# Opening chain, riding routing products, zero fill and first layer norm of an attention, expert and feed-forward kernel

## The chip, the cores and the metric

One core of a Trainium2 chip. The metric is the device time of one execution in microseconds (us). The kernel before was run three times: 1099.04, 1099.73 and 1099.8 us, median 1099.73.

## What is computed

Sparse attention on q, k, v of shape (4, 8, 576, 64), then a mixture of experts in which a token keeps the expert of the one before it, then a layer norm and a feed-forward layer with a residual:

```python
scores = scale * np.matmul(q, k.transpose(0, 1, 3, 2))
thresh = np.max(scores, axis=-1, keepdims=True) - tau
scores = np.where(scores >= thresh, scores, -1000000000.0)
...
            if s == 0 or local_gate[b, s] < 0.5:
                e = fresh_e
            else:
                e = prev_e if prev_e >= 0 else fresh_e
...
            h = np.maximum(x[b, s] @ w1[e], 0.0)
            out[b, s] = p[e] * (h @ w2[e])
...
    xn = (x - mu) / np.sqrt(var + 1e-06) * g_ln
    ch = np.maximum(xn @ w_ch1, 0.0) @ w_ch2
    return (x + ch).astype(np.float32)
```

`x` is the output of attention, laid out as (4, 576, 512). There are 8 experts with weights of 512 x 1024 and 1024 x 512, and the feed-forward layer is 512 x 2048 and back.

## The kernel before

The order of every engine's work is the order in which the program issues it (of the constants ahead of the loads, an order that a scheduler chose; with the change, as issued there too). All products are made of halves: a float is split into two half-precision parts, and three or four matmuls of the parts stand for one.

**Attention** runs over 16 pairs of heads (`p`), 4 pairs to a batch, with 9 items (`j`) to a pair: 144 items of 128 rows of keys or queries. One pass of the main loop (`while it < NI or later`) takes one item through several stages at once. Item `g = it + 13` gets its row maximum (`mx`, on DVE, from scores that `s_mm` put into PSUM); when all nine of a pair have theirs, `th_parts` (POOL) and `th_rows` (PE, ACT) turn maxima into thresholds; item `it + 1` gets the transposed scores less the threshold (`t_mm`, PE, into a tile `s`), item `it` its exponential (`ex`, ACT), item `it - 1` the comparison with the threshold (`mask`, DVE) and the split into halves (`hilo`, ACT and POOL); `pv` multiplies with v, `norm` divides, `store` writes to `x_d` in DRAM. What else is to happen stands in the table `later`, by the number of the pass (`at`): loads, scaling and splitting of the next q and k (`scale_qk`, `split_qk`), their DMA transpose (`prep_t`), the copy `ku` with the halves exchanged (`prep_u`), and the **weight steps**: 11 of the 16 pieces of the feed-forward weights are loaded, narrowed on DVE, scaled on ACT and split, one piece in two halves to a pair (`ffn_steps`, `FO`).

**Routing.** After a pair, `gate` transposes its output and multiplies it with the gate weights, through the one PSUM bank `ps_t`; after the fourth pair of a batch `route` follows, some 30 small DVE instructions with four small products on PE between them (`row`, `kb`, `R`, `A`), each in the same bank. `step_bg` advances this by two steps a pass. As `th_rows` wants the same bank, `settle` runs whatever holds it to its end first.

**The experts** begin while the last batch is routed: `early_work` does a unit "a" of tokens of the first three batches. A **unit** is one or two tiles of 128 tokens of one expert: `gather`, `t_unit` (transposes), `s1_unit` twice or four times (first product, ReLU), `s2_unit` (second product, scaled into `yb` and scattered into `ys_d` with its row number). `ys_d` is filled with zeros beforehand (L1119 to L1126). Weights come in pieces of 512 KB through five buffers `stg`: `more` issues the load, `drip` has ACT and DVE split a loaded piece. After the units of the eight experts come six dynamic ones (`u` from 8 on).

**The feed-forward layer** works on 256 rows at a time: `f_load`, `f_norm`, `f_split`, `f_x` (a DMA transpose on ACT's queue that gives `nT`), then `halve`, which does `f_1` eight times or `f_2` twice, between the dynamic units and then on its own to the end.

Engines: PE multiplies, DVE and ACT work from PSUM and SBUF, POOL from SBUF; SP issues most DMAs.

## Time and profile before

| What | Value |
|---|---|
| Median of three runs | 1099.73 us |
| The profiled execution's own time | 1096.08 us |
| Its span | 1094.3 us |
| Busy share of the span: PE, DVE, ACT, POOL | 92%, 59%, 46%, 36% |
| Granted clock of PE, mean | 0.958 |

Times in a profile count from the span's start. A busy time says that an engine had an instruction running; the arrow behind a row of the timeline names what ended the idle time before it. [...] SPq, ACTq and POOLq are the queues of an engine that issue DMAs; their duration is that of the issuing, not of the transfer. [...]

### The profile page before, as it was taken

How to read it: one execution, taken by the hardware profiler on the slowest of the kernel's cores; microseconds unless marked ns; L12 is line 12 of the kernel's file. 1: busy time of each engine (PE TensorE's matmuls, PEld its weight loads, DVE VectorE, ACT ScalarE, POOL GpSimd, SP SyncE). 2: the span in 40 equal slices, each digit the busy share in tenths (PEclk: the TensorE clock that was granted, in tenths of full speed). 3: DMA queues.
4: the chain of work that ended last, by engine and by line, in shares of the span. 5: the costliest groups of instructions: out<-in, count | busy, mean ns of one | idle time of the engine just before them, and what ended most of it. 6: DMA issues, size and time to landing. Idle time of an engine off the chain costs nothing. (4 is left out here: it accounts for less than half of the span.)

```text
span 1094.3 us, 23622 instructions
## 1 busy us (share of the span) xinstructions
PE 1003.1 (92%) x9888; PEld 738.5 (67%) x9888; DVE 644.8 (59%) x1130; ACT 505.3 (46%) x792; POOL 393.1 (36%) x403
## 2 busy tenths in 40 slices
PE   3799997999799896799999979999999999999995
PEld 1477885788588775576677658576677577576572
DVE  4698889799876852879778767456231231231220
ACT  3587885788477563455567545344111021121110
POOL 4498986789587572025122220100100000000000
PEclk9899998999799997699999989999999999999998
DMA  7546535454433029768879876556011111111100
GB/s 174 144 105 177 146 96 137 107 148 111 107 69 70 21 50 231 237 205 277 270 255 323 259 240 203 151 161 172 25 40 40 30 50 39 30 49 40 29 11 22
DMA packets 126917, 138.23 MB, mean 126 GB/s; under 512 B 69706, under 2 KB 91210, under 8 KB 126800
## 3 DMA queue, kind: packets, MB, share of 16 engines
q1 hardware_dynamic: 101536, 117.71, 38.3%
q0 software_dynamic: 4960, 14.17, 3.6%
q10 hardware_dynamic: 20304, 4.74, 2.5%
q8 instruction: 79, 1.29, 0.5%
q14 instruction: 38, 0.31, 0.1%
HBM read 100.17 MB, written 19.94 MB: 110 GB/s over the span
## 5 line engine op out<-in xcount | busy, mean ns | idle before, releaser
L438 POOL TENSOR_TENSOR hl<-em,hl 128x576 f16<-128x576 f32 x128 | 169.9, 1329 | 58.8 <-ACT hl L437 52.2
L1030 PE MATMUL a<-nT,fw 128*128 128x256 f16 x1728 | 190.1, 273 | 0.0
L1043 PE MATMUL y<-fw,hid 128*128 128x512 f16 x864 | 187.9, 379 | 0.0
L1030 PEld LDWEIGHTS <-fw 128*128 128x128 f16 x1728 | 169.1, 98 | 21.5
L1043 PEld LDWEIGHTS <-hid 128*128 128x128 f16 x864 | 84.5, 98 | 100.4
L138 DVE SCALAR_TENSOR_TENSOR w<-stg,w 128x1024 f16<-128x1024 f32 x112 | 134.2, 1221 | 26.5 <-ACT w L137 17.0
L425 ACT ACTIVATE e<-s,t 128x576 f32<-128x576 f32 x144 | 106.2, 737 | 83.8 <-PE s L420 82.5
L1033 ACT ACTIVATE hid<-a 128x512 f16<-128x512 f32 x72 | 42.7, 593 | 212.7 <-PE a L1030 210.9
L1048 POOL DMA_INDIRECT out_dram<-xf x18 | 18.9, 1051 | 311.9 <-DVE xf L1047 311.9
L942 PE MATMUL y<-w,hid 128*128 128x512 f16 x528 | 120.2, 385 | 6.6 <-ACT hid L925 5.7
L921 PE MATMUL a<-xT,w 128*128 128x128 f16 (+1 forms) x1536 | 124.0, 243 | 2.1 <-DVE w L138 0.9
L382 DVE TENSOR_REDUCE mc<-sm 128x1 f32<-128x576 f32 x140 | 105.1, 751 | 34.7 <-PE sm L378 33.8
L137 ACT ACTIVATE w<-stg 128x1024 f16<-128x1024 f32 x112 | 114.6, 1051 | 18.3 <-DMA x_d<-xc 8.9
L921 PEld LDWEIGHTS <-w 128*128 128x128 f16 x1536 | 114.2, 100 | 12.5 <-issue 1.6
L431 DVE SCALAR_TENSOR_TENSOR em<-s,e 128x576 f32<-128x576 f32 x144 | 107.5, 747 | 20.5 <-POOL hl L438 13.2
L378 PE MATMUL sm<-qkt 128*128 128x288 f16 (+1 forms) x312 | 81.4, 306 | 34.3 <-DMA qkt<-nat 17.3
L1034 DVE SCALAR_TENSOR_TENSOR hid<-a,hid 128x512 f16<-128x512 f32 x72 | 49.6, 688 | 100.0 <-ACT hid L1033 100.0
L1047 DVE SCALAR_TENSOR_TENSOR xf<-y,xf 128x512 f32<-128x512 f32 x18 | 12.5, 692 | 146.8 <-PE y L1043 146.8
L942 PEld LDWEIGHTS <-hid 128*128 128x128 f16 x528 | 51.6, 99 | 68.2 <-ACT hid L925 6.6
L437 ACT ACTIVATE hl<-em 128x576 f16<-128x576 f32 x128 | 87.0, 679 | 21.3 <-DVE em L431 20.8
L415 PE MATMUL s<-qkt 128*128 128x288 f16 (+1 forms) x320 | 92.9, 298 | 3.6 <-DVE em L431 3.3
L378 PEld LDWEIGHTS <-qkt 128*128 128x128 f16 (+1 forms) x640 | 58.3, 109 | 56.2 <-issue 21.3
(272 smaller groups left out, 1840.3 us busy)
## 6 DMA issues: line engine op xcount, KB each, us to landing
stg<-in_moe_w_dram SPq DMA_DIRECT2D x112, 512.0 KB
stg<-in_moe_w_ch_dram SPq DMA_DIRECT2D x32, 512.0 KB
ys_d<-zero SPq DMA_DIRECT2D x2, 2308.5 KB
xf<-ys_d SPq DMA_DIRECT2D x9, 513.0 KB
ku<-qkt SPq DMA_DIRECT2D x30, 144.0 KB
rawq<-in_q_dram SPq DMA_DIRECT2D x8, 512.0 KB
rawk<-in_k_dram SPq DMA_DIRECT2D x8, 512.0 KB
vraw<-in_v_dram SPq DMA_DIRECT2D x8, 512.0 KB
```

Source lines behind the costliest of these rows:

```text
L137: nc.scalar.activation(out=dst[:, 0, n], in_=t, func=AF.Copy, scale=scale)
L138: nc.vector.scalar_tensor_tensor(out=dst[:, 1, n], in0=t, scalar=scale, in1=dst[:, 0, n], op0=ALU.mult, op1=ALU.subtract)
L378: mm(o[:, W0 + 288 * c:W0 + 288 * c + 288], ops[p, "q"][0][:, n], y, start=(k == 0), stop=(k == 1))
L382: nc.vector.tensor_reduce(out=mcs[p % 2][:, j:j + 1], in_=mms.pop((p, j))[:, W0:W0 + 576], op=ALU.max, axis=AX.X)
L415: mm(o[:, W0 + 288 * c:W0 + 288 * c + 288], (kt, ku)[k][:, n], y, start=(k == 0), stop=False)
L425: nc.scalar.activation(out=e, in_=mst[p, j][:, W0:W0 + 576], func=AF.Exp, bias=t0, scale=SC)
L431: nc.vector.scalar_tensor_tensor(out=em, in0=ps[:, W0:W0 + 576], scalar=0.0, in1=e, op0=ALU.is_ge, op1=ALU.mult)
L438: nc.gpsimd.tensor_tensor(out=hl[:, 1], in0=em, in1=hl[:, 0], op=ALU.subtract)
L921: nc.tensor.matmul(ps[:, f, :], t1[:, a, c, fc], x[:, h, i:i + N // 128, c, :], start=(n == 0), stop=(n == 11))
L942: nc.tensor.matmul(ps, hid[:, x, f, 128 * i:128 * i + 128], t2[:, a, f, :], start=(n == 0), stop=(n == 23))
L1030: nc.tensor.matmul(ps[:, f, :], fw1[:, a, c, fc], x[:, h, :, c, :], start=(n == 0), stop=(n == 11))
L1043: nc.tensor.matmul(ps, hid[:, x, f, ts_], fw2[:, a, f, :], start=(n == 0), stop=(n == 47))
```

## The change

*Opening.* q and k of the first pair alone are loaded first, k on ACT's queue (`load_pair`); constants are made on POOL instead of DVE, and the memsets stand behind the loads (`blanks`, new; its lines were in the setup before); 14 matmuls of ones run meanwhile; `start_qk` splits k on DVE and q on ACT and DVE, and PE transposes both. The loop starts with 9 passes of lead, and in four passes of pair 0 a second maximum is taken, which brings the lead to 13. `th_parts(0)` is on DVE. Pair 1 still goes through a DMA transpose, and its `ku` is copied on DVE.

```diff
+    ctx.enter_context(tc.manual_schedule())
...
+        def load_pair(nm, n, e):
+
+            src = {"q": q, "k": k, "v": v}[nm][0]
+            e.dma_start(
+                out=raws[nm][:, n].rearrange("p (h r) d -> p h (r d)", h=2)[:, :, 0:4 * D],
+                in_=src[2 * n:2 * n + 2, 0:512].rearrange("h (p r) d -> p h (r d)", r=4))
...
-            if p:
+            if p > 1:
...
+
+        def start_qk():
+
+            V = nc.vector
+            nat = tr_p.tile([128, 18, 128], F16, name="qkt")
+            scale_qk(0, "q", False)
+            rq, rk = (raws[nm][:, 0, 0:9] for nm in "qk")
+            V.tensor_scalar(out=rk, in0=rk, scalar1=16.0, scalar2=None, op0=ALU.mult)
+            nc.scalar.activation(out=nat[:, 0:9, 0:64], in_=rq, func=AF.Copy)
+            V.tensor_copy(out=nat[:, 9:18, 0:64], in_=rk)
+            V.tensor_tensor(out=nat[:, 9:18, 64:128], in0=rk, in1=nat[:, 9:18, 0:64], op=ALU.subtract)
+            V.tensor_tensor(out=nat[:, 0:9, 64:128], in0=rq, in1=nat[:, 0:9, 0:64], op=ALU.subtract)
+            for nm in "qk":
+                scale_qk(1, nm, False)
+                split_qk(1, nm)
+            t = tr_p.tile([128, 18, 128], F16, name="qkt")
+            for nm, o in (("k", 9), ("q", 0)):
+                ps = ps_s.tile([128, 2048], F16, name="s")
+                for i in range(9):
+                    nc.tensor.transpose(ps[:, 128 * i:128 * i + 128], nat[:, o + i, :], ident16)
+                d = t[:, o:o + 9].rearrange("p a b -> p (a b)")
+                if nm == "k":
+                    V.tensor_copy(out=d, in_=ps[:, 0:1152])
+                    ops[0, "k"] = d
+                else:
+                    nc.scalar.activation(out=d, in_=ps[:, 0:1152], func=AF.Copy)
+                    ops[0, "q"] = (d, d)
+            prep_u(0)
+            prep_t(1)
...
-            ps = (ps_s if p == 0 and j % 2 else ps_m).tile([128, 1024], F32, name="s" if p == 0 and j % 2 else "sm")
+            two = p == 0 and JO.index(j) % 3
+            ps = (ps_s if two else ps_m).tile([128, 1024], F32, name="s" if two else "sm")
...
-            G = nc.gpsimd
+            G = nc.gpsimd if p else nc.vector
```

*Riding products.* For all batches but the last, `route` is no longer run by `gate`: it hands each of its four products out, `ride` puts that into the unused first 224 columns of the tile `s` of the next item, right behind `t_mm`, and `alight` goes on with it when that item is masked. Where nothing rides, a pass advances the route by one step. The other products (`kb`, `R`, `A`) are changed as `row` is. The weight steps leave out the pairs 6 and 10 and end in pair 12 or 13. The zero fill goes from two writes in pass 135 to six from pass 124 on, from a buffer of the weight steps.

```diff
-                yield
-                yield from route(b)
+                if b < B - 1:
+                    routes.append([route(b), None])
+                else:
+                    yield
+                    yield from route(b)
...
+            inner = b < B - 1
+
+            def product(f):
+                if inner:
+                    got = yield f
+                else:
+                    got = bank(b).rearrange("p a b -> p (a b)")
+                    f(got)
+                return got
+
+            def rest():
+                if not inner:
+                    yield
...
-            row = bank(b).rearrange("p a b -> p (a b)")[0:1, 0:192]
-            nc.tensor.matmul(row[:, 0:128], loc[:, 3:4], ident16)
-            nc.tensor.matmul(row[:, 128:192], key[0:64, 4:5], ident16[0:64, 0:64])
+            def f_row(t):
+                nc.tensor.matmul(t[0:1, 0:128], loc[:, 3:4], ident16)
+                nc.tensor.matmul(t[0:1, 128:192], key[0:64, 4:5], ident16[0:64, 0:64])
...
             V.tensor_scalar(out=sm, in0=sm, scalar1=1e-9, scalar2=2.0 ** -15, op0=ALU.add, op1=ALU.mult)
-            yield
+            row = (yield from product(f_row))[0:1, 0:192]
+            yield from rest()
             holdr = T("holdr", [1, 192])
             V.tensor_scalar(out=holdr, in0=row, scalar1=0.0, scalar2=None, op0=ALU.is_equal)
...
-            close()
...
-        LEAD = 13
-        bgp, held = [], []
+        LEAD, FIRST = 13, 9
+        bgp, held, routes = [], [], []
...
+        def step_route(got=None):
+
+            r = routes[0]
+            try:
+                r[1] = r[0].send(got)
+            except StopIteration:
+                routes.pop(0)
+
+        def ride(p, j):
+
+            if routes and callable(routes[0][1]):
+                t = mst[p, j][:, 0:W0]
+                routes[0][1](t)
+                routes[0][1] = (p, j, t)
+
+        def alight(p, j):
+            if routes and isinstance(routes[0][1], tuple) and routes[0][1][:2] == (p, j):
+                step_route(routes[0][1][2])
...
+        soon = {
+            1: ((12, prep_u), (4, scale_v), (2, split_v)),
+            2: ((22, scale_qk, "q", False), (20, split_qk, "q"), (20, scale_qk, "k"), (19, split_qk, "k"), (18, prep_t), (16, prep_u), (4, scale_v), (2, split_v)),
+        }
+        at(-6, scale_v, 0)
+        at(-5, split_v, 0)
         for p in range(npair):
             if p:
-                for lead, f, *a in prep:
+                for lead, f, *a in soon.get(p, prep):
                     at(9 * p - lead, f, p, *a)
-            at(9 * p - 4, th_parts, p)
-            at(9 * p - 2, th_rows, p)
+                at(9 * p - 4, th_parts, p)
+                at(9 * p - 2, th_rows, p)
...
-        for w in range(FA):
+        for w, slot in enumerate((0, 1, 2, 3, 4, 5, 7, 8, 9, 11, 12)):
...
-                    at(max(0, 9 * w + o), st)
+                    at(max(-1, 9 * slot + o), st)
+        def zero(n):
+
+            if n == 0:
+                P["zero"] = cv_p.tile([128, 512, 2], I32, name="stg").rearrange("p a b -> p (a b)")[:, 0:DM + 1]
+                nc.vector.memset(P["zero"][:, 0:DM], 0)
+                nc.vector.memset(P["zero"][:, DM:DM + 1], BIG)
+            h = NT // 6
+            nc.sync.dma_start(
+                out=ys_d[h * n:h * n + h, :].rearrange("(t p) d -> p t d", p=128).bitcast(I32),
+                in_=P["zero"].unsqueeze(1).to_broadcast([128, h // 128, DM + 1]))
+
+        for n in range(6):
+            at(124 + 2 * n, zero, n)
```

*Opening and loop, as issued; zero fill and gather at the end of attention.*

```diff
-        yb = P["u_p"].tile([128, DM + 1], F32, name="yb")
+        yb = P["u_p"].tile([128, DM + 1], F32, name="yb", bufs=2)
...
+        nc.vector.memset(ones16, 1.0)
+        nc.vector.memset(c16, 1.0)
+        load_pair("q", 0, nc.sync)
+        load_pair("k", 0, nc.scalar)
+        nc.sync.dma_start(out=t0, in_=tau.unsqueeze(0).to_broadcast([128, 1]))
+        for part in (2, 3):
+            load(0, "q", part)
+            load(0, "k", part, nc.scalar)
+        warm = ps_t.tile([128, 4, 128], F32, name="t")
+        for i in range(14):
+            mm(warm, ones16, ones16.unsqueeze(1).to_broadcast([128, 4, 128]))
+        nc.scalar.activation(out=c16, in_=c16, func=AF.Exp)
+        nc.vector.memset(vraw[:, :, 4:6, :], 0.0)
+        nc.vector.tensor_copy(out=ident16, in_=ident)
+        load_pair("q", 1, nc.sync)
+        load_pair("k", 1, nc.sync)
+        load_pair("v", 0, nc.sync)
+        for part in (2, 3):
+            load(0, "v", part)
+        load_pair("v", 1, nc.sync)
         for nm in "qkv":
             load(0, nm, 1)
...
+        constants()
+        start_qk()
...
-        it = -LEAD
+        it = -FIRST
+        g = -1
+        ahead = {0: 2, 2: 2, 4: 2, 5: 2}
...
+            g += 1
...
+                alight(*items[it - 1])
...
+            if it == -1: th_parts(0)
             if g + 1 < NI: s_mm(*items[g + 1])
+            if it == -1: th_rows(0)
...
-            if 0 <= it + 1 < NI: t_mm(*items[it + 1])
+            if 0 <= it + 1 < NI:
+                t_mm(*items[it + 1])
+                ride(*items[it + 1])
...
+            if ahead.get(it):
+                g += 1
+                mx(*items[g])
+                s_mm(*items[g + 1])
...
-                zero = P["um_p"].tile([128, DM + 1], F32, name="zero")
-                nc.gpsimd.memset(zero, 0.0)
-                nc.gpsimd.memset(zero.bitcast(I32)[:, DM:DM + 1], BIG)
-                for n in range(2):
-                    h = NT // 2
-                    nc.sync.dma_start(
-                        out=ys_d[h * n:h * n + h, :].rearrange("(t p) d -> p t d", p=128),
-                        in_=zero.unsqueeze(1).to_broadcast([128, h // 128, DM + 1]))
-            if it == 9 * (npair - 1) + 1: gather("a")
+            if it == 9 * (npair - 1) + 7: gather("a")
...
+            if routes and routes[0][1] is None and len(bgp) < 2: step_route()
```

*First normalising*, and two buffers `yb` (above). It moves from dynamic unit 8 into unit 9.

```diff
             for k in range(2):
                 s1_unit(u, k)
+                if i == 1:
+                    if late:
+                        next(late.pop(), None)
+                    (f_norm, f_split)[k](0)
                 drip(1)
             if i + 1 < ND0:
                 t_unit(u + 1)
+                if i == 1:
+                    f_x(0)
                 if i + 3 < ND0:
                     gather(u + 3)
             s2_unit(u, 0, lambda: drip(2))
-            if i == 0:
-                f_norm(0)
-                f_split(0)
-                f_x(0)
```

How instructions move. First, DVE in the opening, from the last maxima of pair 0 (`mc`) to the first masks (`em`); `ku`, `r` and `pt` are the exchanged copy and the thresholds' parts. Before:

```order
L382 TENSOR_REDUCE mc<-sm 128x1
L382 TENSOR_REDUCE mc<-s 128x1
L382 TENSOR_REDUCE mc<-sm 128x1 x6
L431 SCALAR_TENSOR_TENSOR em<-s,e 128x576
L382 TENSOR_REDUCE mc<-sm 128x1
L431 SCALAR_TENSOR_TENSOR em<-s,e 128x576
L155 TENSOR_SCALAR cv<-stg 128x512
```

Now:

```order
L403 TENSOR_REDUCE mc<-s 128x1 x2
L412 TENSOR_SCALAR r<-mc,taus 128x12
L413 CAST pt<-r 128x12
L414 TENSOR_TENSOR r_393<-r,pt 128x12
L415 CAST pt<-r_393 128x12
L416 TENSOR_TENSOR pt<-r_393,pt 128x12
L403 TENSOR_REDUCE mc<-sm 128x1 x2
L1234 TENSOR_SCALAR g_84<-g_84 128x4
L403 TENSOR_REDUCE mc<-sm 128x1
L452 SCALAR_TENSOR_TENSOR em<-s,e 128x576
L403 TENSOR_REDUCE mc<-sm 128x1
```

Six maxima of pair 1 stood ahead of the first mask, now three; the copies for pair 1 and the thresholds' parts are new in this queue.

Second, DVE in the routing of the first batch, from the operand of the first product (`loc`) to its first reader (`holdr`). Before:

```order
L562 SCALAR_TENSOR_TENSOR loc<-hold,key 128x4
L564 TENSOR_REDUCE smx<-ex_3011 128x5
L569 TENSOR_SCALAR smx<-smx 128x5
L382 TENSOR_REDUCE mc<-sm 128x1
L431 SCALAR_TENSOR_TENSOR em<-s,e 128x576
L572 TENSOR_SCALAR holdr<-t 1x192
L573 RECIPROCAL smx<-smx 128x5
L574 SCALAR_TENSOR_TENSOR erow<-holdr,t 1x192
L580 TENSOR_TENSOR ex_3011<-ex_3011,smx 128x40
```

Now, from five rows behind `loc` on:

```order
L146 SCALAR_TENSOR_TENSOR cv<-stg,cv 128x512
L608 TENSOR_SCALAR smx<-smx 128x5
L403 TENSOR_REDUCE mc<-sm 128x1
L452 SCALAR_TENSOR_TENSOR em<-s,e 128x576
L403 TENSOR_REDUCE mc<-sm 128x1
L489 TENSOR_SCALAR rd<-o 128x5
L491 RECIPROCAL rd<-rd 128x5
L452 SCALAR_TENSOR_TENSOR em<-s,e 128x576
L493 TENSOR_TENSOR xc<-o,rd 128x5x64
L403 TENSOR_REDUCE mc<-sm 128x1
L452 SCALAR_TENSOR_TENSOR em<-s,e 128x576
L612 TENSOR_SCALAR holdr<-s 1x192
```

There was one mask between operand and reader, and there are four (one stands ahead of the piece shown); the reader takes the product from the tile `s` in place of the bank `t`. In the whole listing the routing instructions of this batch stood between the 52nd and the 58th mask, and stand now between the 51st and the 69th.

Third, ACT around the first layer norm (`sq`, `f` and the transpose to `nT`) in the dynamic units; `hid` is the result of a unit's half, `w` a weight piece. Before:

```order
L137 ACTIVATE w_10282<-stg 128x1024 x2
L948 ACTIVATE yb<-y,tp 128x512
L994 ACT_TABLE_LOAD
L994 ACTIVATE sq<-ve 128x2
L1009 ACTIVATE f_10417<-xn 128x512 x2
L1016 DMA_TRANSPOSE nT<-f_10417 128x16x128
L925 ACTIVATE hid<-a 128x4x128 x2
L192 ACTIVATE fw_143<-xn 128x512
```

Now:

```order
L1039 ACTIVATE yb<-y,tp 128x512
L1016 ACTIVATE hid<-a 128x4x128
L1085 ACT_TABLE_LOAD
L1085 ACTIVATE sq<-ve 128x2
L1016 ACTIVATE hid<-a 128x4x128
L179 ACTIVATE fw_97<-xn 128x512
L1100 ACTIVATE f_10561<-xn 128x512 x2
L124 ACTIVATE w_10570<-stg 128x1024
L988 ACTIVATE xT<-a 128x512
L1107 DMA_TRANSPOSE nT<-f_10561 128x16x128
L124 ACTIVATE w_10570<-stg 128x1024 x2
```

The two evictions `hid` of unit 9 stood behind the transpose and stand now ahead of it; one of them, a weight piece and the next unit's `xT` are between the square root and the transpose.

## Rows read from the trace of the kernel before

**Rows 1.** Busy time by stretch; columns: stretch, its us, engines, PEclk, DMA share, GB/s.

```profile
5.00:10.00 5.00, 0.00 (x0) 0.00 (x0) 2.31 (x27) 1.74 (x3) 1.69 (x2) 1.00 1.17 251
104.50:126.60 22.10, 21.59 (x315) 18.07 (x315) 19.41 (x32) 18.24 (x31) 20.10 (x20) 1.00 0.54 133
172.10:206.60 34.50, 27.56 (x330) 21.67 (x330) 29.00 (x62) 18.68 (x32) 20.84 (x20) 0.80 0.44 102
274.40:308.60 34.20, 27.52 (x329) 21.65 (x330) 29.04 (x62) 18.45 (x31) 20.76 (x20) 0.80 0.41 90
330.50:351.70 21.20, 21.19 (x315) 17.96 (x315) 14.46 (x25) 15.87 (x27) 16.10 (x18) 1.00 0.26 56
373.00:399.90 26.90, 22.25 (x301) 18.27 (x302) 20.86 (x56) 14.49 (x23) 13.99 (x16) 0.87 0.05 13
430.00:440.00 10.00, 0.36 (x2) 0.36 (x3) 2.40 (x5) 2.50 (x3) 0.00 (x0) 0.61 0.94 323
440.00:450.00 10.00, 9.05 (x67) 7.89 (x66) 6.89 (x17) 4.68 (x8) 0.00 (x0) 0.50 0.97 298
500.00:550.00 50.00, 50.00 (x390) 35.75 (x389) 39.23 (x48) 29.26 (x39) 14.33 (x14) 1.00 0.87 291
```

**Rows 2.** Waits of PE from 172 to 207 us, longest first (total, times, longest).

```profile
PE t L567 <- DVE loc L562: 3.0, 1, 3.0
```

**Rows 3.** Timeline of the opening (start us, us, engine, line, operation).

```profile
7.44 0.77 ACT L308 ACTIVATE rawq<-rawq,qs 128x576 f32<-128x576 f32 x1 [4.69 <-DMA rawq<-in_q_dram]
...
9.72 0.68 ACT L308 ACTIVATE rawk<-rawk 128x576 f32<-128x576 f32 x1 [0.80 <-DMA rawk<-in_k_dram]
...
12.50 2.88 SPq L319 DMA_TRANSPOSE qkt<-nat  x1
...
17.27 0.45 PE L378 MATMUL sm<-qkt 128*64 128x288 f16 x1 [17.27 <-DMA qkt<-nat]
...
17.72 0.45 DVE L332 COPY ku<-qkt 64x1152 f16<-64x1152 f16 x1
...
26.16 0.28 PE L378 MATMUL sm<-qkt 128*128 128x288 f16 x1
...
27.62 0.75 DVE L382 TENSOR_REDUCE mc<-s 128x1 f32<-128x576 f32 x1
...
30.33 0.45 PE L378 MATMUL sm<-ku,qkt 128*64 128x288 f16 x1 [2.29 <-DMA ku<-qkt]
```

**Rows 4.** Timeline, from the thresholds' rows to the first exponential.

```profile
37.20 1.06 PE L403 MATMUL t<-identb,pt 128*128 128x128 bf16 x8
...
41.03 0.74 ACT L425 ACTIVATE e<-s,t 128x576 f32<-128x576 f32 x1 [2.13 <-PE s L420]
```

**Rows 5.** Timeline of SP's queue, weight loads behind the zero writes.

```profile
405.34 13.68 SPq L212 DMA_DIRECT2D stg<-in_moe_w_dram  x2
```

**Rows 6.** Timeline, end of attention, ACT and DVE.

```profile
436.45 2.18 ACT L137 ACTIVATE w<-stg 128x1024 f16<-128x1024 f32 x2 [8.88 <-DMA x_d<-xc]
437.54 1.23 DVE L138 SCALAR_TENSOR_TENSOR w<-stg,w 128x1024 f16<-128x1024 f32 x1 [9.14 <-DMA stg<-in_moe_w_dram]
438.68 0.16 DVE L468 TENSOR_SCALAR rd<-o 128x5 f32<-128x5 f32 x1
```

**Rows 7.** Timeline around the first layer norm, units 8 and 9.

```profile
637.41 5.34 PE L942 MATMUL y<-w,hid 128*128 128x512 f16 x24
...
642.59 5.52 PE L921 MATMUL a<-xT,w 128*128 128x128 f16 x96
...
644.56 1.29 DVE L987 BATCH_NORM_STATS2 st<-xf 128x6 f32<-128x512 f32 x2 [1.72 <-DMA xf<-ys_d]
...
651.47 2.10 ACTq L1016 DMA_TRANSPOSE nT<-f  x1
...
654.27 7.11 PE L942 MATMUL y<-w,hid 128*128 128x512 f16 x24 [5.71 <-ACT hid L925]
...
661.21 7.04 PE L1030 MATMUL a<-nT,fw 128*128 128x256 f16 x63
```

More of the change, by code (lines that the diff above doesn't have):

```diff
@@ L310, in split_qk @@
         def split_qk(p, nm):
+            if p not in pending:
+                pending[p] = nat_p.tile([128, 18, 128], F16, name="nat")
             r = raws[nm][:, p % NP, 0:9]
@@ L622, in route, with f_A @@
             yield
-            A = bank(b).rearrange("p a b -> p (a b)")[:, 0:4 * E]
-            for i in range(5):
-                M = 128 if i < 4 else 64
-                for a in range(2):
-                    nc.tensor.matmul(A, ol[0:M, i], ov[0:M, i, 2 * a:2 * a + 2].rearrange("p a b -> p (a b)"), start=(i + a == 0), stop=(i + a == 5))
-            yield
+            def f_A(t):
+                for i in range(5):
+                    M = 128 if i < 4 else 64
+                    for a in range(2):
+                        nc.tensor.matmul(t[:, 0:4 * E], ol[0:M, i], ov[0:M, i, 2 * a:2 * a + 2].rearrange("p a b -> p (a b)"), start=(i + a == 0), stop=(i + a == 5))
+            A = (yield from product(f_A))[:, 0:4 * E]
+            yield from rest()
             ac = acc.rearrange("p a b -> p (a b)")
@@ L633, in route @@
                 V.tensor_tensor(out=ac, in0=A, in1=ac, op=ALU.add)
-            close()
+            if not inner: close()
             if b == B - 2:
```

204 lines of the change are left out of this document (97 added, 107 removed).

## Prediction

> **What bounds the kernel now.** I read the table of windows first, cut at the first exponential of a pair. An ordinary pair of heads takes 22.1 us, with the matrix engine (PE) busy for 21.59 of them; a pair without weight steps takes 21.2 with PE busy for 21.19. So attention runs at PE's pace, and DVE (19.41 of 22.1 busy) is close behind. Two pairs stand out: 34.5 and 34.2 us, with PE busy for only 27.5 and a granted clock of 0.80; a third takes 26.9. They are the pairs in which a batch is routed. Then 430 to 440 us, in which PE does 0.36 us of work, and ten more at half clock. From 500 us on PE is busy for 50.00 of 50 us: what is saved ahead of that is saved at the end, unless something there is late [rows 1]. The list of waits says why the routing pairs are long: PE stands at a routing product whose operand DVE has not made yet (3.0 us in one piece) [rows 2], and as PE works in order, scores and products with v stand behind it.
>
> The timeline then shows three other holes. The opening: the first score matmul is at 17.27, the first exponential at 41.03 [rows 3, 4]. The end of attention: behind two writes of zeros (4.7 MB by their shape) on SP's queue the weight loads are issued from 405.34 on, two of them in 13.68 us [rows 5]; the first weight piece is split at 436.45 on ACT and 437.54 on DVE, and the last normalising of attention, at 438.68, stands behind that split in DVE's queue [rows 6]. And the first layer norm: PE stands for 5.71 us ahead of 654.27 [rows 7].
>
> **The change part by part.** The sum is made against the profiled execution (span 1094.3, its own time 1096.08). The median of the runs shown is 1099.73, that is 3.65 us more, and I carry that over.
>
> *Opening.* q is scaled at 7.44 and k at 9.72; a DMA transpose is issued at 12.50 and its result used at 17.27; nine maxima end at 27.62 + 0.75 = 28.37; then four items of pair 1 must have their scores (PE waits for them until 30.33) before the thresholds' matmuls come at 37.20; 3.83 us later stands the exponential [rows 3, 4]. Now q and k of pair 0 alone come first, on two queues. 0.5 MB less must arrive ahead of k, which is 2.0 us at 251 GB/s [rows 1], and k's issue no longer waits for q's: both are ready at some 7.0 (estimate; the memsets on DVE end about then too). Then three DVE passes over 576 columns at 0.76 each (priced like a maximum of that width) = 2.3, nine PE transposes about 1.0, the copy of 1152 columns out of PSUM about 1.5 (twice the 0.75 of 576), two copies at 0.46 = 0.9. First score: 12.7. The nine items take the 11.1 us that they take now (17.27 to 28.37), which gives 23.8; the thresholds' parts, five small instructions that move from POOL to DVE, 1.0 (0.16 for the small one at 438.68 [rows 6], and the way between two), and 3.8 as now: first exponential at 28.6, which is 12.4 earlier. Less sure is the other pair's operand: pair 1's DMA transpose is queued behind all loads of batch 0 (3.5 MB, 14 us at 251 GB/s, so it lands near 21), and DVE copies from it between the seventh and eighth maxima. That is just in time. Given back: the four items that no longer lead are caught up in pair 0, 4 x 0.76 = 3.0 us of DVE beside an engine that is nearly full. **Net -9.4.** Bounds: -2 (pair 1 and pair 2 operands late by 4 us each), -13.5 (the nine items at 0.75 each, DVE's pace). The constants that move to POOL and the memsets have 7 us of loading over them and cost nothing; without that cover they would cost about 3.
>
> The clock is what makes the nine items slow: a 288-column matmul takes 0.45 at 17.27, 0.28 at 26.16, and 0.45 again at 30.33, where PE had stood for 2.29 us [rows 3]. The fourteen warm-up matmuls end before the operands are ready, so I take the slow pace again. [...]
>
> *Riding products.* The order shows each batch's four products behind a score group, three items apart, and DVE's routing work spread over items 51 to 69 instead of 52 to 58. Their operands are made an iteration ahead, behind nothing long, and their readers stand behind the mask, which waits for the same score group anyway. So PE's stalls go. What stays is DVE work: 29.0 - 19.41 = 9.6 us for one batch [rows 1], now over two pairs, 4.8 each. A pair without weight steps has 14.46 of DVE; with 4.8 it has 19.3, as an ordinary pair does, and those take 22.1. The pause in the weight steps is a little shorter than the routing, so I put the routing pairs at 22.4. Savings: 34.5 - 22.4, 34.2 - 22.4 and 26.9 - 21.7 make 29.1; the two pairs that now get weight steps cost 0.9 each (22.1 - 21.2). **Net -27.5.** Bounds: -3 (all 9.6 us of DVE on the path, twice, and pair 14 unchanged) and -31 (every such pair at 21.2).
>
> *Zero fill and the end of attention.* Six writes of 0.77 MB go out two items apart, in a stretch in which the DMA share is 0.05 [rows 1]; each takes some 3 us at 251 GB/s, of the 4.5 between two. Nothing but stores of attention output stands behind them on SP's queue, and those are read much later. The weight loads then start at once, ten items before they are needed. The order on DVE is the same: split, then normalise; but the split no longer waits. PE's hole of 10.3 us closes (0.36 us of work from 430 to 440, and a little beside), and the following 9.05 us of work at half clock [rows 1] take less: 4.5 if PE alone decided there. In the routing of the last batch DVE decides part of it, so I take 2.7. **Net -13.** Bounds: -6 (the sixteen weight pieces of the first unit arrive no faster than it uses them) and -17. The gather that moves six items later has five items to land in, no cost; the second yb buffer frees a POOL-ACT pair that nothing waits for, no cost.
>
> *First normalising.* Moved behind the first half of the next unit, it starts later and is cut up. Now: DVE starts at 644.56, and the DMA transpose goes out right behind its last instruction, at 651.47: 6.9 us. Then: the half unit ends at 642.59 + 2.76, its eviction at about 646.8; 6.9 us of normalising make 653.7, and the order puts a narrowing and an eviction between, some 3 us: 656.5 to 657. A DMA transpose takes 4.8 us for 2304 columns (12.50 to 17.27) [rows 3], say 4.3 for 2048: nT is there at 661. PE is done with what it can do at 642.59 + 5.52 + 5.34 and four small transposes, about 654, and the next thing in its order needs nT. So the hole does not go: it moves from ahead of the unit's second product to behind it, and the FFN starts at 661 as now (661.21). Behind the hole the first FFN matmuls run at half clock, as the 24 products now do (7.11 against 5.34, 1.8 us) [rows 7]. **Net +2.** Bounds: -3.3 (nothing between, 657.9) and +4.
>
> Sum: -9.4 - 27.5 - 13 + 2 = -47.9: 1048.2 for the profiled execution, **1052 for the median**.
>
> **The rivals.**
> - *The normalising hole goes.* If the transposed tile is there when the second product ends, 5.7 us of idling and 1.8 of slow clock go, -7.5 in place of +2: 1042. For it: PE has five more microseconds of work ahead of the hole. Against: DVE's and the DMA's own 11 us start 2.2 us later.
> - *The early operands or weights are late.* The opening gives only 2 (pair 1's or pair 2's transposes behind loads), or the end of attention only 6: 1059, both 1066. For it: SP's queue puts 3.5 MB ahead of pair 1's transpose. Against: it has until the eighth maximum.
> - *The clock stays up* from the warm-up through the first nine items: the nine items at DVE's pace of 0.75 in place of 1.1 each, 1049. Against: the row at 30.33 [rows 3], and no row here speaks for it. [...]
> - *The rides stall PE.* Slower: a product stands in PE's order behind a score group, so if its operand is late, the next scores wait, twelve times. At the price of the two settled places of a routing pair now, (34.5 - 22.1) / 2 = 6.2 us, that is 74 us in place of nothing: 1126. It decides from 48 / 12 = 4.0 us a ride. Against: the operand is made an item (2.4 us) ahead.
>
> That the products do not ride is excluded by the order, in which they write the score tile.
>
> **How the numbers follow.** Forecast 0.47, hole gone 0.12, late operands or weights 0.22, clock 0.15, stalled rides 0.03, nothing to be seen 0.01. The forecast's own errors (3 us for the opening, 4 for riding, 4 for the end of attention, 2 for the normalising) make 7 to 8 together; with the first two rivals the range is 1036 to 1071. A measurement of this kernel can tell 0.2%, some 2 us, from no change: faster 0.96, same 0.01, slower 0.03.
>
> **What would show it.** First exponential at 28 to 29 and pair 0 some 3 us longer than now; no pair above 23.5; no PE gap over 3 us between the last exponential and 500; a PE gap of 4 to 7 us behind the second product of the second dynamic unit. Wrong if a routing pair stays above 26, if the first weight split still waits, or if the FFN follows without a gap.

## The result and the profile after

The changed kernel takes 1066.99 us (median of 4 runs, 1065.47 to 1068.27); the kernel before took 1099.38 on the same chip. The ratio is 0.9707, 95% interval 0.9691 to 0.9724. Forecast were 1052 and 1036 to 1071: faster, inside the range, but 15 us too good. The profiled execution has a span of 1065.0 us and a time of 1066.93 of its own.

Cutting both traces at the same points shows where the span's 29.3 us come from. "Start" of a pair is its first exponential.

| stretch | before | after | change | forecast |
|---|---|---|---|---|
| up to the start of pair 2 | 81.4 | 73.1 | -8.3 | -9.4 |
| start of pair 2 to start of pair 15 | 318.5 | 300.4 | -18.1 | -27.5 |
| start of pair 15 to the first expert product | 41.0 | 34.8 | -6.3 | -13 |
| first expert product to the end | 653.3 | 656.8 | +3.5 | +2 |

The first expert product, which divides the last two lines, is at 440.99 and 408.25. The normalising lies wholly behind it. Of the +3.5, 1.6 arose ahead of the first product of the feed-forward layer (FFN), 661.21 and 630.11, and 1.8 behind it. Of the -18.1, 1.0 is pair 2, which has no routing.

The table of windows of the changed kernel, cut at the starts of pairs; columns are the stretch, its length, busy time of PE, PE's weight load, DVE, ACT and POOL (instructions in brackets), the granted share of PE's full clock (PEclk), DMA share, GB/s:

```profile
139.30:165.30 26.00, 21.78 (x315) 18.14 (x316) 23.70 (x43) 18.60 (x32) 21.80 (x22) 1.00 0.47 109
165.30:188.00 22.70, 22.29 (x326) 18.62 (x326) 18.65 (x42) 17.31 (x30) 17.40 (x20) 1.00 0.41 110
188.00:211.70 23.70, 22.13 (x325) 18.57 (x324) 21.62 (x39) 17.43 (x29) 17.04 (x17) 1.00 0.52 123
233.80:261.00 27.20, 23.07 (x316) 19.11 (x317) 24.89 (x44) 18.53 (x33) 22.88 (x22) 0.94 0.49 120
261.00:283.20 22.20, 22.05 (x325) 18.54 (x325) 17.30 (x40) 17.04 (x29) 16.21 (x18) 1.00 0.34 92
...
391.60:408.20 16.60, 12.20 (x145) 10.34 (x141) 6.23 (x13) 6.85 (x11) 5.76 (x5) 0.74 0.26 75
408.20:430.00 21.80, 17.57 (x142) 13.27 (x142) 17.79 (x48) 10.51 (x14) 0.57 (x1) 0.66 0.72 228
```

The pairs that took 34.5, 34.2 and 26.9 [rows 1] take 22.7, 22.2 and 21.0 (165.3, 261.0, 352.5): the rides do what they were meant to. But the pairs ahead of two of them now take 26.0 and 27.2 (23.4 and 23.3 before) with DVE busy for 23.70 and 24.89, and the pairs behind these two 23.7 and 23.8. The hole of 430 to 440 [rows 1] is gone, yet from 391.6 to 430 PE's clock is 0.74 and 0.66. The first pair of them in the kernel before:

```profile
148.70:172.10 23.40, 21.65 (x314) 17.94 (x313) 21.15 (x35) 18.54 (x33) 21.42 (x21) 1.00 0.49 118
```

The places of the routing's 33 DVE instructions say where its work went: 11 stand in pair 5, 15 in pair 6 and 7 in pair 7, and only pair 6 is without weight steps. Before it was 4 in pair 5 and 29 in pair 6.

What fills the long pair, in the timeline (start, length, engine, line and operation, out<-in; in square brackets idle time and what ended it). First DVE, then POOL, then PE:

```profile
156.82 0.83 DVE L592 SCALAR_TENSOR_TENSOR eq<-eq,iota 128x40 f32<-128x40 f32 x1
...
157.92 0.94 DVE L596 SCALAR_TENSOR_TENSOR key<-idx,fr 128x5 f16<-128x5 f32 x1
158.90 1.21 DVE L598 TENSOR_SCALAR hold<-key 128x4 f32<-128x4 f16 x1
160.14 1.27 DVE L600 TENSOR_TENSOR_SCAN loc<-hold,key 128x4 f16<-128x4 f32 x1
161.33 0.18 DVE L602 TENSOR_REDUCE smx<-ex 128x5 f32<-128x40 f32 x1
161.43 0.74 DVE L403 TENSOR_REDUCE mc<-sm 128x1 f32<-128x576 f32 x1
```

```profile
156.32 1.28 POOL L459 TENSOR_TENSOR hl<-em,hl 128x576 f16<-128x576 f32 x1
157.56 1.29 POOL L306 TENSOR_TENSOR nat<-rawk,nat 128x576 f16<-128x576 f32 x1
158.80 1.28 POOL L459 TENSOR_TENSOR hl<-em,hl 128x576 f16<-128x576 f32 x1
160.03 1.36 POOL L363 TENSOR_TENSOR vl<-vraw,vh 128x640 f16<-128x640 f32 x1
```

```profile
162.22 0.28 PE L399 MATMUL sm<-qkt 128*128 128x288 f16 x1 [3.11 <-DVE mc L403]
```

Four of DVE's small routing instructions take 0.83 to 1.27 us for 4 to 40 columns. Each ends within 0.06 of the end of a POOL instruction: 157.65 beside 157.60, 158.86 beside 158.84, 160.11 beside 160.08, 161.41 beside 161.39. A fifth (line 608, at 164.08) takes 1.25. Three of the five (lines 592, 596 and 600) read two operands in SBUF; lines 598 and 608 read one. The reductions among them, with one operand, take 0.18 to 0.20. The next maximum, at 161.43, is late by these waits, and PE stands for 3.11 us. In the last routing, when attention is over and POOL idles, the same lines are short:

```profile
416.27 0.20 DVE L592 SCALAR_TENSOR_TENSOR eq<-eq,iota 128x40 f32<-128x40 f32 x1
...
416.73 0.17 DVE L596 SCALAR_TENSOR_TENSOR key<-idx,fr 128x5 f16<-128x5 f32 x1
...
417.14 0.17 DVE L600 TENSOR_TENSOR_SCAN loc<-hold,key 128x4 f16<-128x4 f32 x1
```

Added up over all its 33 DVE instructions, a routing takes 7.4 us there (start of the first at 415.8, end of the last at 428.5), 14.3 beside the pairs, and 12.6 in the kernel before.

### The profile page after: what moved, and what is told of

Same layout as the page of the kernel before. It is cut to its first block, busy times and chain, and to the rows that moved or that the text cites. A ratio compares the mean times of both kernels' runs of the same rounds, so it can differ in the third digit from the quotient of the medians.

```text
span 1065.0 us, 23705 instructions
## 1 busy us (share of the span) xinstructions
PE 999.8 (94%) x9920; PEld 735.2 (69%) x9920; DVE 653.1 (61%) x1127; ACT 506.1 (48%) x791; POOL 390.2 (37%) x411
## 5 line engine op out<-in xcount | busy, mean ns | idle before, releaser
L1121 PE MATMUL a<-nT,fw 128*128 128x256 f16 x1728 | 192.5, 274 | 6.3 <-DMA nT<-f 6.3
L1121 PEld LDWEIGHTS <-fw 128*128 128x128 f16 x1728 | 170.1, 98 | 29.3 <-issue 6.8
L403 DVE TENSOR_REDUCE mc<-sm 128x1 f32<-128x576 f32 x138 | 103.6, 751 | 24.4 <-PE sm L399 22.4
L399 PE MATMUL sm<-qkt 128*128 128x288 f16 (+1 forms) x308 | 75.4, 291 | 24.4 <-DVE mc L403 21.3
L436 PE MATMUL s<-qkt 128*128 128x288 f16 (+1 forms) x320 | 90.6, 291 | 4.2 <-DVE em L452 3.2
L441 PE MATMUL s<-th,ind 128*128 128x128 bf16 (+5 forms) x960 | 92.6, 207 | 0.0
```

Source lines behind the costliest of these rows:

```text
L403: nc.vector.tensor_reduce(out=mcs[p % 2][:, j:j + 1], in_=mms.pop((p, j))[:, W0:W0 + 576], op=ALU.max, axis=AX.X)
L436: mm(o[:, W0 + 288 * c:W0 + 288 * c + 288], (kt, ku)[k][:, n], y, start=(k == 0), stop=False)
L441: mm(o[:, W0 + i:W0 + i + w], ind[:, t % 4, 0:o.shape[0]], y, start=False, stop=(i == of[-1][0]))
L1121: nc.tensor.matmul(ps[:, f, :], fw1[:, a, c, fc], x[:, h, :, c, :], start=(n == 0), stop=(n == 11))
```

## The experiments

In the timed runs the kernel before took 1095.2 to 1099.4 us from one set of runs to another, the changed kernel 1067.0 and 1066.7; so ratios of different sets differ by 0.003 with nothing changed, and medians are compared with 1066.7 to 1067.0 here.

**POOL idle at the start of a routing.** In six items, and for one low half of k and one of v, ACT writes zeros where POOL subtracts; twice.

```diff
-            nc.gpsimd.tensor_tensor(out=hl[:, 1], in0=em, in1=hl[:, 0], op=ALU.subtract)
+            if 9 * p + JO.index(j) in [36 * b + 51 + n for b in (0, 1) for n in range(6)]:
+                nc.scalar.activation(out=hl[:, 1], in_=hl[:, 0], func=AF.Copy, scale=0.0)
+            else: ...
```

> Against the changed kernel's 1067.0 us. Left out in six items around the start of the first two routings: the low halves of the masked exponentials, of k and of v, which ACT fills with zeros there, so that POOL stands idle. Theory (POOL holds up DVE): the routing's small instructions that read two operands in SBUF end when the POOL instruction beside them ends (0.83, 0.94, 1.21, 1.27 and 1.25 us where an undisturbed one takes 0.17 to 0.20); with POOL idle they take 0.2, pairs 5 and 9 fall from 26.0 and 27.1 us to 22 to 23, and the time to 1058 to 1060. Rival (DVE is simply full there, since weight steps and routing meet): the small instructions stay long or DVE stays behind, pairs 5 and 9 stay above 25, time 1065 to 1068.

1066.1 us. Pairs 5 and 6 took 24.3 and 24.4, together what they took before (48.7). The small instructions were short:

```profile
160.12 0.17 DVE L605 SCALAR_TENSOR_TENSOR key<-idx,fr 128x5 f16<-128x5 f32 x1
...
160.53 0.17 DVE L609 TENSOR_TENSOR_SCAN loc<-hold,key 128x4 f16<-128x4 f32 x1
```

So the waits are POOL's, but ACT, with eight instructions of some 0.68 more, was busy almost without a break from 154.8 to 166 and was late itself. As to the time, this run tells nothing apart.

**POOL writes only.** The same places, but POOL writes zeros (0.58 us, no operand read).

```diff
+                nc.gpsimd.memset(hl[:, 1], 0.0)
```

> Against the changed kernel's ratio to the kernel before, 0.9707. Left out at the start of the first two routings: the same low halves (of six masked exponentials, of k and of v, each twice), in whose place POOL writes zeros, so that ACT gets no extra work this time. Theory (POOL's reading instructions hold up DVE): the routing's small instructions take 0.2 us, pairs 5 and 9 take 22 to 23 us (26.0 and 27.1 in the changed kernel) and pairs 6 and 10 stay at 22 to 23; 8 us less, ratio 0.962 to 0.965. Rival (DVE is full there): pairs 5 and 6 together stay at 48 to 49, as pairs 9 and 10, ratio 0.969 to 0.973.

1061.7 us, 5 less than the changed kernel. Pairs 5 and 9 took 24.5 and 24.4, pairs 6 and 10 22.3 each: the sum falls by 1.9 and 2.6 us (by 2.9 each against the changed kernel's second profile), which the rival excluded. It is not the 22 to 23 that I expected, and the rows say why: one instruction still meets a subtraction, another the memsets.

```profile
158.30 0.84 DVE L601 SCALAR_TENSOR_TENSOR eq<-eq,iota 128x40 f32<-128x40 f32 x1
...
159.41 0.17 DVE L605 SCALAR_TENSOR_TENSOR key<-idx,fr 128x5 f16<-128x5 f32 x1
159.61 1.62 DVE L607 TENSOR_SCALAR hold<-key 128x4 f32<-128x4 f16 x1
161.27 0.17 DVE L609 TENSOR_TENSOR_SCAN loc<-hold,key 128x4 f16<-128x4 f32 x1
```

```profile
157.80 1.28 POOL L468 TENSOR_TENSOR hl<-em,hl 128x576 f16<-128x576 f32 x1
159.02 0.58 POOL L307 MEMSET nat<- 128x576 f16 x1
159.54 0.58 POOL L466 MEMSET hl<- 128x576 f16 x1
160.06 0.63 POOL L367 MEMSET vl<- 128x640 f16 x1
160.63 0.58 POOL L466 MEMSET hl<- 128x576 f16 x1
```

What is left of waits is 0.6 and 1.5 us, and the pair is 2.4 over 22.1; with 4.6 us of waits it was 3.9 over (5.1 in the second profile). The pairs behind, 7 and 11, stayed at 23.8 with POOL untouched there.

**Routing three items later.**

```diff
+        def later_route(b):
+            for _ in range(3 if b < B - 2 else 0):
+                yield
+            yield from route(b)
```

> Against the changed kernel's 1067.0 us. The first two routings start three items later; nothing is left out. Theory (POOL holds up DVE): their small instructions then meet one POOL instruction an item and not five in a row, and the weight steps pause there: pairs 5 and 9 at 22.1, pairs 6 and 10 at 22.5 to 23.5, time 1058 to 1062. Rival (the work itself does not fit beside a pair): what leaves pairs 5 and 9 comes back in pairs 6, 7, 10 and 11, time 1065 to 1069.

1074.7 us, slower by 8, more than either expected. Pairs 5 and 9 took 22.1, but 6, 7, 10 and 11 took 28.7, 27.3, 27.5 and 27.3: nearly the rival's picture. Other small instructions of the chain now met POOL, and a routing took 14.9 us on DVE:

```profile
162.96 1.11 DVE L588 SCALAR_TENSOR_TENSOR fr<-lg,first 128x5 f32<-128x5 f32 x1
...
164.10 1.15 DVE L593 TENSOR_TENSOR ex<-lg,mxl 128x40 f32<-128x40 f32 x1
```

On top of it the clock fell (0.88 in pair 6). After 1.95 us of idling, four score matmuls took 1.12 us where they take 0.65.

**Small instructions on POOL itself.**

```diff
+                G.tensor_scalar(out=eq, in0=eq, scalar1=-64.0, scalar2=None, op0=ALU.mult)
+                G.tensor_tensor(out=eq, in0=eq, in1=i8, op=ALU.add)
+                yield
...
+                G.tensor_tensor(out=key, in0=idx, in1=fr, op=ALU.mult)
+                G.tensor_scalar(out=hold, in0=key[:, 0:4], scalar1=0.0, scalar2=None, op0=ALU.is_equal)
```

> Against the changed kernel's ratio, 0.9707. Four of the five small instructions of the first two routings go to POOL itself, where they queue behind its long ones and not beside them; nothing is left out, and the first product rides two items later. Theory (POOL holds up DVE): DVE is freed of some 4 us a routing and POOL gets 6 instructions of 0.25; pairs 5 and 9 at 22.1 to 23, ratio 0.963 to 0.966. Rival (POOL, with 21.8 of 26 us busy there, becomes late, and the low halves with it): PE waits for low halves, pairs 5 and 9 stay at 25 or more, ratio 0.969 to 0.974.

1066.0 us: nothing gained. Pairs 5 and 9 fell to 22.7 as the theory says, but 6 and 10 rose to 27.6 and 25.8, 7 and 11 to 24.9 and 24.8. DVE now stood in order behind POOL's results (first two rows), and two items later three other small instructions met POOL's next row of long ones (last three):

```profile
164.60 0.20 DVE L602 TENSOR_REDUCE idx<-eq 128x5 f32<-128x40 f32 x1 [1.90 <-POOL eq L600]
...
167.77 0.17 DVE L609 TENSOR_TENSOR_SCAN loc<-hold,key 128x4 f16<-128x4 f32 x1 [1.55 <-POOL hold L606]
...
183.39 1.36 DVE L640 TENSOR_TENSOR_SCAN e<-hold,s,key 128x4 f32<-128x4 f32 x1
184.78 1.24 DVE L642 SCALAR_TENSOR_TENSOR oh<-iota,e 128x40 f16<-128x40 f32 x1
186.06 1.20 DVE L649 TENSOR_TENSOR ex<-ex,oh 128x40 f32<-128x40 f32 x1
```

**POOL's long instructions moved away.**

```diff
+                    if p in (8, 12) and a == ["k"]:
+                        lead += 2
+                    if p in (6, 10, 14) and f in (scale_v, split_v):
+                        lead -= 5
```

> Against the changed kernel of the same call. POOL's long instructions are moved off the start of a routing: the low half of k for pairs 8 and 12 two items earlier, that of v for pairs 6, 10 and 14 five items later; DVE's order stays as it is, nothing is left out. Theory (POOL holds up DVE): of the five long instructions in a row two go, so the small ones wait 1 to 2.5 us in place of 4.6; pairs 5 and 9 at 23 to 24.5, 5 to 8 us less together, ratio 0.005 to 0.007 lower. Rival (DVE is full there, whatever POOL does): pairs 5 and 9 at 26 to 27, ratio within 0.002.

1068.1 us (0.9754, 0.9738 to 0.977, beside 0.9734 for the changed kernel): no gain. Pairs 5 and 9 took 24.7 and 24.8, a little over the expected 23 to 24.5; pairs 6 and 10 rose to 24.5, and the moved half of v now stands beside later routing instructions (lines 627 and 634 took 1.12 and 0.91), and a routing took 15.1 us of DVE. Five runs agree: the waits follow POOL's long instructions. POOL is busy for 16 to 23 us of such a pair, and the chain of 33 small instructions met them in each of the orders tried.

**Zero fill as before.**

```diff
-        for n in range(6):
-            at(124 + 2 * n, zero, n)
...
+                for n in range(2):
+                    h = NT // 2
+                    nc.sync.dma_start(out=ys_d[h * n:h * n + h, :]..., in_=zero2...)
```

> Against the changed kernel's 1067.0 us. The zero fill alone is put back: two writes at the start of the last pair. Theory (the zero fill held up the weight loads, and a slow clock and POOL's gather ate the rest of its gain): PE's hole ahead of the first expert unit is 9 to 11 us again instead of 1.7, and what this hides (two waits of PE for the low halves, 2 us) is saved: 1072 to 1076. Rival as in the prediction (the term was the full 13): 1080. Rival (the loads came early for another reason): 1066 to 1068, first weight split without a wait.

1076.2 us. From the last exponential to the first expert product it took 24.1 us (16.7 and 15.5 in the changed kernel's two profiles); the hole came back in two parts, 7.3 in place of the expected 9 to 11, the gathered rows and the weights both being late:

```profile
408.24 2.32 PE L985 MATMUL a<-ident,xg 128*128 128x128 f32 x8 [3.66 <-DMA xg<-x_d,etb]
...
417.29 1.12 PE L530 MATMUL a<-ident,xc 128*128 128x128 f32 x4 [3.67 <-DVE xc L493]
```

So the zero fill is worth 7.4 to 8.6 us there, not 13, and not nothing, with the gather where the change has it: in the kernel before the gather was issued six items earlier, and no run puts both back. (The profile is 10.7 longer; some 3 of it arose earlier, 2.4 in pair 2.)

**Gather behind the last low half.**

```diff
-            if it == 9 * (npair - 1) + 7: gather("a")
+            if it == 9 * (npair - 1) + 9: gather("a")
```

> Against the changed kernel's ratio, 0.9707. The gather of the first expert unit is issued two items later, behind POOL's last low half. Theory (its two issues, 1.26 and 1.02 us on POOL, stand ahead of the last two low halves and make PE wait 1.07 and 0.88 us): these two waits go, the first expert product comes 1.5 to 2.5 us earlier, ratio 0.968 to 0.970. Rival (the gathered rows then arrive late): PE waits at the transposes of the gathered rows, ratio 0.971 to 0.974.

1065.2 us, 1.5 to 1.8 less, about the spread of the runs. In the changed kernel two issues on POOL stand ahead of the last two low halves, and PE waits for both:

```profile
392.76 1.26 POOL L904 DMA_INDIRECT xg<-x_d,etb  x1 [0.18 <-POOL hl L459]
394.32 1.02 POOL L904 DMA_INDIRECT xg<-x_d,etb  x1 [0.30 <-issue]
```

```profile
396.70 0.23 PE L476 MATMUL o<-vh,hl 128*128 128x65 f16 x1 [1.07 <-POOL hl L459]
...
397.93 0.24 PE L476 MATMUL o<-vh,hl 128*128 128x65 f16 x1 [0.88 <-POOL hl L459]
```

With the gather later, these waits were gone, but PE now waited 0.34 and 0.80 us for the gathered rows, the rival's picture in part. The first expert product came 15.9 us after the last exponential. That shows no gain: the changed kernel itself took 16.7 in one profile and 15.5 in the other, with both waits for POOL in each (1.05 and 0.96 in the second).

**First normalising as before**, run twice.

```diff
             s2_unit(u, 0, lambda: drip(2))
+            if i == 0:
+                f_norm(0)
+                f_split(0)
+                f_x(0)
```

> Against the changed kernel's 1067.0 us. The first normalising alone is put back, behind the first dynamic unit. Theory as in the prediction (the hole only moves, and the slow clock after it then falls on FFN products): 1 to 4 us faster than the changed kernel, 1063 to 1066. Rival (the move saved part of the hole): 1069 to 1073, with PE idle for more than 6.4 us ahead of the FFN's first product or of the unit's second one.

> Against the changed kernel of the same call. The first normalising alone back behind the first dynamic unit, as in the earlier run of it (1060.6 against 1065.0 in the profiles, but 0.9721 against 0.9707 in ratios of two chips). Theory as in the prediction (the move costs 2): 1 to 4 us faster, ratio 0.001 to 0.004 lower. Rival (it moves nothing that can be told): within 0.001.

1064.4 and 1065.5 us, against 1067.0 and 1066.7; the second time 0.9726 (0.9712 to 0.974) against 0.9734 (0.972 to 0.9748), so the times alone don't separate them. Nor do the whole spans (1060.6 and 1061.0 against 1065.0 and 1064.7), since in both runs the profiled execution was the fastest of its kernel. The stretch that the edit touches does: from the FFN's first product to the end it takes 432.4 and 432.9 us, 433.1 in the kernel before, and 434.2 to 435.7 in all ten profiles with the normalising moved. Counted from the first expert product it is 652.4 and 652.8 against 656.8 and 656.5. The clock behind the FFN's start says why: 1.00 with the normalising put back, 0.50 with it moved (630.00:634.00 further below).

```profile
628.10:634.00 5.90, 5.90 (x55) 5.28 (x54) 2.75 (x3) 2.67 (x4) 1.02 (x1) 1.00 0.79 302
```

The sign of the theory is borne out. By the two pairs of profiles the move costs 3.7 to 4.4 us, at the upper end of the expected 1 to 4; by the medians 1.2 to 2.6.

**Two edits in the opening.**

```diff
+            for nm, o in (("q", 0), ("k", 9)):
+                n = pending[1][:, o:o + 9]
+                V.tensor_tensor(out=n[:, :, 64:128], in0=raws[nm][:, 1, 0:9], in1=n[:, :, 0:64], op=ALU.subtract)
...
+            behind = g < NI and bool(ahead.get(it - 1)) and it > 0
+            if g < NI and not behind: mx(*items[g])
...
+            if behind: mx(*items[g])
```

> Against the changed kernel's ratio, 0.9707. Two edits in the opening: the low halves of pair 1's q and k are made on DVE behind pair 0's two copies, so that POOL stands idle beside these copies (1.18 and 1.44 us where such a copy takes 0.46), and in an item behind a caught-up maximum the next maximum comes behind the mask and not ahead of it (DVE waits 0.67 to 0.74 us for the score there, four times). Theory: the copies take 0.46, the first maximum starts 1 to 1.5 us earlier, pair 0 takes 21 to 22 us in place of 23.9; 3 to 4 us less, ratio 0.967 to 0.968. Rival (pair 1's operands then set the opening, or PE's clock paces pair 0): no more than 1 us, ratio 0.970 to 0.971.

1066.6 us: the rival. In the changed kernel the two copies behind pair 0's transposes stand beside POOL:

```profile
10.03 1.18 DVE L322 COPY ku<-qkt 64x1152 f16<-64x1152 f16 x1
11.22 1.44 DVE L323 COPY ku<-qkt 64x1152 f16<-64x1152 f16 x1
```

```profile
9.61 1.28 POOL L306 TENSOR_TENSOR nat<-rawq,nat 128x576 f16<-128x576 f32 x1 [3.37 <-ACT nat L305]
10.89 1.45 POOL L306 TENSOR_TENSOR nat<-rawk,nat 128x576 f16<-128x576 f32 x1
```

In the experiment they took 0.46 each, but the first score then waited for ACT's copy of q (12.10), and the first exponential stayed at 27.8. Pair 0 fell from 23.9 to 22.9, so the order of maximum and mask is worth 1.0 there, and the start of pair 2 fell from 73.1 to 72.0.

**Control, and all together.** The changed kernel again, and one with POOL's instructions moved, the gather later, the normalising back and the opening's edits.

> The changed kernel itself, on the same chip as the three that follow. Both theories: ratio 0.969 to 0.973; it says how far ratios of different chips may be compared, and how often pair 2 (23 to 24.5 us in six of seven kernels since, 22.1 in the profile of the changed kernel) waits for its operand: with 1 to 2 us more there the profile shows PE waiting for the transfer that fills pair 2's second copy of k.

> Against the changed kernel of the same call. POOL's long instructions moved, the first normalising back, the gather behind the last low half, and the two edits of the opening, together. Theory: the sum of 5 to 8, 1 to 4, 1 to 2 and 1 to 1.5 us: ratio 0.958 to 0.965. Rival (one of them takes back what another gives, since a stall of PE moves to the next late engine): ratio 0.966 or more.

Control 1066.7 us (0.9734, 0.972 to 0.9748); all together 1063.5 (0.9699, 0.9682 to 0.9717). It is 3.2 us faster than the changed kernel, the intervals do not touch, and it is the fastest here that computes everything. The profiles put the gain in one edit, the normalising: up to the first expert product the combination is 0.7 us later than the control (408.9 and 408.2), and from there on 3.2 shorter (653.3 and 656.5). The expected 0.958 to 0.965 was missed: the moved instructions gave nothing, the later gather nothing that can be told, and pair 15 grew to 19.1. As to pair 2: in the control its fifth item took 3.60 us (3.27 in the first profile), in eight of the other kernels 3.5 to 5.3; in the longest PE waited 0.90 us for the transfer of k's second copy.

## Why the prediction was right, and where it was 15 us off

Sign and range were right, and the places too: rides, opening and end of attention all gain. Against the profiled execution the sum should have been 47.9 and was 29.3. By its steps:

- **Riding products, -27.5 against -18.1: the step that failed.** The three pairs came out as forecast (22.7, 22.2 and 21.0 for 22.4, 22.4 and 21.7). Wrong was "29.0 - 19.41 = 9.6 us for one batch", spread as "4.8 each" over two pairs, and with it the nothing that the sum holds for the pairs around. The window that I subtracted begins at 172.1 [rows 1], and the routing's first instructions stand ahead of it, from 165.8 on; over the whole routing it was 12.6. Nor are two pairs enough: the items 51 to 69 of the order reach from pair 5 into pair 7, and 18 of the 33 instructions lie in these two, which keep their weight steps. And the 12.6 is no fixed amount: 7.4 alone, 14.3 beside pairs in which POOL is busy. Nor does it spread evenly, since the five long instructions, 5.5 us, come within two items. So pairs 5, 9 and 13 grew by 2.6, 3.8 and 2.2 us and pairs 7 and 11 by 1.3 and 2.0 (up to 0.9 of pair 11's is the weight steps, priced in the forecast). My bound of -3 covers it. POOL's subtractions are shown as a cause by the run in which memsets of some 0.6 us stand in their place, which gave back 4.5 us (5.8 against the second profile) of the first two routings; the rest of the shortfall is not taken apart. (The step's own sum is 29.1 less 1.8, that is 27.3 and not 27.5.) Beside POOL's subtractions the instructions with two operands of lines 596 and 600 took 0.94 and 1.27 us, where 0.17 is usual, and that of line 605 in the run in which POOL writes only took 0.17 beside a memset (159.41). Why the comparison of line 598, with one operand, took 1.21 us no row shows.
- **Zero fill and the end of attention, -13 against -6.3.** The hole ahead of the first expert unit fell from 10.82 us (10.3 in the prediction) to 1.71, and the zero fill alone is worth 7.4 to 8.6. The 2.7 for less work at half clock did not come: PE stood again, and the stretch from 408.25 to 421.72 took 13.47 us as before (440.99 to 454.47), at a granted clock of 0.57 (0.56 before). And "five items to land in, no cost" looked at the gather's landing and left out its two issues on POOL, ahead of the last low halves: 2 us of PE's waits, though taking them away moved the first expert product by nothing that can be told. What still stops PE is DVE's order, in which a split of a weight stands ahead of the last normalising. The hole before, and the rows now:

```profile
439.64 1.12 PE L509 MATMUL a<-ident,xc 128*128 128x128 f32 x4 [10.82 <-DVE xc L472]
```

```profile
404.80 1.23 DVE L125 SCALAR_TENSOR_TENSOR w<-stg,w 128x1024 f16<-128x1024 f32 x1 [0.24 <-ACT w L124]
405.94 0.16 DVE L489 TENSOR_SCALAR rd<-o 128x5 f32<-128x5 f32 x1
```

```profile
406.90 1.12 PE L530 MATMUL a<-ident,xc 128*128 128x128 f32 x4 [1.71 <-DVE xc L493]
```

- **Opening, -9.4 against -8.3.** First exponential at 27.92 (forecast 28.6), first score at 11.89 (12.7). Eighteen transposes took 1.35 (the 1.0 for nine had no row), and DVE's copy of 1152 columns out of PSUM 0.76 and not 1.5. Pair 0 grew by 5.1 and not by 3.0: a caught-up maximum costs 0.76 us and, 0.67 to 0.74 each, a wait for its score, since two maxima in a row find the second score not ready (of these waits the run with the mask ahead took back 1.0). No row shows a wait for the constants on POOL, as forecast; the low halves that POOL makes beside DVE's copies cost these copies 1.7 us, most of it hidden behind ACT's copy of q.
- **First normalising, +2 against +3.5.** The mechanism was right: the gap is behind the second product, and the clock after it is 0.50. The size was not, since the FFN's start did not stay: from the first expert product to it takes 221.9 us in place of 220.2, and 220.0 and 220.0 with the normalising put back. PE waits 0.84 us inside the second product for a result that DVE hands over late, a wait that the prediction puts at nothing, and the gap is 6.35 and not 5.71. My bound of +4 covers it:

```profile
621.21 2.55 PE L1033 MATMUL y<-w,hid 128*128 128x512 f16 x11 [0.84 <-DVE hid L1017]
630.11 10.15 PE L1121 MATMUL a<-nT,fw 128*128 128x256 f16 x70 [6.35 <-DMA nT<-f]
```

```profile
630.00:634.00 4.00, 3.89 (x19) 2.73 (x20) 1.10 (x1) 0.23 (x1) 1.02 (x1) 0.50 0.83 267
634.00:638.00 4.00, 4.00 (x34) 3.37 (x33) 1.85 (x2) 1.65 (x3) 0.00 (x0) 0.88 0.39 146
```

- **The 3.65 us** between the profiled execution and the median, carried over from the kernel before, are not there after (1066.93 and 1066.99). That the median's error is 15 and not 18.7 is luck.

Of the rivals, "the rides stall PE" fell: between 139 and 212 PE waits for maxima alone, never for a ride. "The clock stays up" fell too: a score matmul takes 0.45 us from 11.89 to 16.9 (the next one starts 0.24 later; granted clock 0.50 from 11.80 to 17.10), and 0.29 only from 17.15 on (0.12 later; 1.00 from 17.15 to 20.00), when half of the nine items are through. In the kernel before, the clock reads 1.00 beside the same 0.45 from 17.20 to 24.00 and 0.50 from 30.30 on, so that the clock made its nine items slow rests on the lengths alone. "Early operands or weights late" is there in part (a last split ahead of a normalising; pair 2 without a wait in the changed kernel, and with 0.60 and 0.90 us of PE waiting for k's second copy in two of the other runs). None named POOL.

Of the signs that I named, the gap ahead of the FFN was there; the first exponential came a little earlier than 28. "No PE gap over 3 us" fails by a wait of 3.20 at 427.30 for a routing operand, which the kernel before has too. "No pair above 23.5" was not there, nor pair 0 "some 3 us longer" (5.1). And a sign of being wrong, "a routing pair stays above 26", came true for pair 9, in which a routing now begins: 27.2.

Open is what a routing would cost with all its small operands out of SBUF, or on other engines: POOL alone was tried. Nor was the nearest rival tried, to leave the weight steps out of pairs 5 and 7 too; so how much of their growth is plain DVE work, and how much POOL, is known for the start of a routing alone. That the falls of the clock behind the stalls cost what the rows suggest was not tried by itself.

## What to carry to other kernels

Before spreading a chain of small DVE instructions through a stretch in which POOL works, compare the same instruction's length beside POOL and alone (here 1.27 and 0.17 us), and count the whole chain, not what of it a window shows. Moving such a chain, or POOL's work, only changed here which instructions meet; a gain came where POOL wrote zeros in place of subtracting (5 us). When an operation is moved later on a queue, look at who stands behind it there: the gather's two issues on POOL were followed by waits of PE of 1.07 and 0.88 us. And before a stretch of one profile is called a gain, look at the same stretch in a second profile of the same kernel: 16.7 and 15.5 us here with nothing changed.

## What the hardware did that I had not expected

With POOL only writing, DVE's instruction with two operands was undisturbed beside a memset (0.17 us, at 159.41 and 251.94 of that run), but the comparison with one 16-bit operand took 1.62 and 1.63 us, through three memsets of POOL in a row and not one.

The same 3.11 us of idling of PE ahead of 162.22 (changed kernel) and of 162.34 (its control) was followed once by a granted clock of 1.00 and once by 0.59 from 163.00 to 166.70: that item took 5.89 and 7.18 us, and pair 5 26.0 and 27.2, with the same instructions.
